# Fetching the next batch's keys and queries one layer earlier, with a third key place and a reordered side schedule, in a fused attention, Fourier-mix and feed-forward kernel

## The chip, the core and the metric

The kernel runs on one core of a Trainium2 chip. A core has five engines that run side by side: TensorE (matmuls and transposes, PE in the profile), VectorE (DVE), ScalarE (ACT), GpSimd (POOL) and SyncE (SP, which here issues most DMA transfers). Each works through its own list of instructions in order and waits for others through semaphores. The metric is the device time of one execution in microseconds.

## The reference

Eight batches of 576 tokens, eight heads of 64 columns. Attention is the linear kind: keys are normalised over the tokens, queries over the columns, and a 64 x 64 product of keys and values stands between them. The result x (576 x 512 per batch) is mixed by a two-dimensional Fourier transform of which the real part is kept; then comes a layer norm and a feed-forward block of two layers (512 to 2048 to 512).

```python
q_s = exp(q - max(q, -1));  q_s = q_s / (sum(q_s, -1) + 1e-9)
k_s = exp(k - max(k, 2));   k_s = k_s / (sum(k_s, 2) + 1e-9)
kv = einsum('bhsd,bhse->bhde', k_s, v)
x = einsum('bhsd,bhde->bhse', q_s, kv)        # then (B,H,S,D) -> (B, S, H*D)
u = x + real(fft(fft(x, axis=1), axis=2))
un = (u - mean(u)) / sqrt(var(u) + 1e-6)
out = u + maximum(un @ w_ch1, 0.0) @ w_ch2
```

## The kernel before

The 576 tokens of a batch are cut into four *own* tiles of 128 tokens, named (c, u) with c and u in 0, 1, and a remainder of 64. The remainders of two batches fill one *shared* tile ("t", b), so even batches have five query tiles and odd ones four. The feed-forward works on nine groups of 512 tokens: the eight batches' own tiles and one group of all shared tiles.

After a start that converts the weights and handles batch 0 and the attention and mixing of batch 1, the program is a list of steps, each with a time in units of the feed-forward's matmul steps. The function `timed` writes eight such **passes** (its argument `order`, 1 to 8). The list is sorted by time, and each engine gets its instructions in that order; nothing reorders them later. Pass n runs the feed-forward of one group and, between its matmuls, the attention, mixing and norm of batch n+1 (passes 1 to 6):

- the first layer (`up`, 56 steps, matmuls at L1171): four jobs of 14 steps. Each uses two weight loads `big<-w1s` of 896 KB. There are four places for streamed weights; `used(n)` says that load n is done with, and issues load n+4 into its place (L449).
- the second layer (`down`, matmuls at L1297 and L1267, 50 steps from pass 2 on): seven-product recursion on blocks; its weights come as `big<-w2d` and `big<-w2s`. The seven products add up in three banks of PSUM, "ba", "bb" and "bc". VectorE forms sums u and s from them (L1141 and L1182 in the first layer, L1304 in the second), and block differences (L1243) that later products read. `single` (L1267) multiplies a unit whole, in two halves i = 0, 1; `add` (L1278) adds a half to x.

Attention of a batch takes four key blocks ("k", b, r). Each is loaded (k by L579 or L585, v by L592 and L593), its maximum taken on VectorE (L620), its exponential on ScalarE (L626), transposed on TensorE (L644, L652), copied to `ks` by ScalarE (L648) and VectorE (L657), and multiplied with v (L669). Keys have two places and values two. The query tiles then follow: load (L696, or four parts and a remainder at L330 and L331 for the shared tile), maximum (L723), exponentials (L729), sums, a multiplication by the reciprocal (L742; tiles with c = u have it after the product instead, at L812), transposes (L750), product (L803), copy to x (L814).

`attention_timed` gives these their times. `start` is 0 in passes 1 and 2 and -7 in passes 3 to 6 (so that the first key is turned before the pass begins), `end` is 45. Key r has its exponential at start + 3.5 r. The own query tiles are spread evenly up to 31.3; their loads stand 6.5 steps ahead. Keys 0 and 1 of the next batch are fetched at the end of `folded`, 12.2 steps after `end`, so at the beginning of the second layer. There a `gate` (L560) follows: a VectorE instruction that writes one element of the new key tile from another tile.

`norm` takes statistics of x (L1005, L1006), a root (L1009), the normalised x (L1034), its transposes (L1040) and copies to `unT` (L1048), and the combinations of `unT` that the recursion of the next pass needs: L398 and L400 on VectorE, L399 on GpSimd, and L401 on VectorE (slot 6).

`store` writes x out. Tiles with c different from u are written through `mirror`, a buffer in DRAM, because their tokens stand in reverse: x to mirror (L1425), and 9 steps later mirror to the output (L1427). Others go directly (L1418).

Of the kernel before, what the change touches and what calls it, by code (L numbers as in the profile page):

```python
# [137 lines left out]
class _Block:  # L138
# [154 lines left out]
    def hold(self):  # L293


        held = {12: [("q", D, 3)] * 3, 15: [("k", S, 2)] * 2 + [("v", NC * P, 2)] * 2}
        for some in held.values():
            for i, (tag, n, bufs) in enumerate(some):
                t = self.work.tile([P, n], F32, tag=tag, name=tag, bufs=bufs)
                self.nc.gpsimd.memset(t[0:1, 0:1], 0.0)  # L300
                some[i] = t[0:1, 0:1]

        def free(f):
            copy = self.nc.vector.tensor_copy
            for t in held.get(f, ()):
                copy(t, self.h0[0:1, f, 0:1])
            if f == 12:

                for w in (self.w1sb[0:1, :, HD::HD], self.w2sb[0:1, 0:4, ::HD]):
                    copy(w, w)  # L310
            if f == NF - 1:
                copy(self.w1sb[0:1, :, 0:1], self.w1sb[0:1, :, 0:1])
        return free
# [183 lines left out]
    def attention_timed(self, b, start, end):  # L497
# [3 lines left out]
        own = [("q", b, c, u) for c in range(2) for u in range(2)]  # L501
        first = start + 14 + 5 * len(tail)
        gap, steps = (end - 13.7 - first) / 3, []
        for i, it in enumerate(keys):
            t = start + 3.5 * i
            steps += at(t - 5.5, self.k_load(it)) + at(t, self.k_exp(it)) + at(t + 4, self.k_turn(it))
            steps += at(t + 7, self.k_times_v(it))
        for it in tail:
            t = start + 14
            steps += at(t - 12, self.t_load(it)) + at(t, self.q_exp(it)) + at(t + 8, self.t_turn(it))  # L510
            steps += at(21 if start < 0 else 35, self.t_fold(it))
        for i, it in enumerate(own):
            t = first + gap * i
            steps += at(t - 6.5, self.q_load(it)) + at(t, self.q_exp(it)) + at(t + 8.7, self.q_turn(it))
            steps += at(t + 11.7, self.q_times_kv(it))
        return steps + at((33 if start < 0 else 39) if tail else 22, self.t_times_kv(b))

# [45 lines left out]
    def k_load(self, it):  # L563
# [9 lines left out]
        if r < 2:  # L573
            return []

        def keys():
            k, v = self.key_places()
            self.live[it] = [k, v]
            self.nc.sync.dma_start(k, self.kT[b, r * P:(r + 1) * P, :])  # L579

        return [(0, keys), (3, lambda: self.values_to(b, r, self.live[it][1]))]

    def keys_to(self, b, r, k, v):
        nc = self.nc
        nc.sync.dma_start(k, self.kT[b, r * P:(r + 1) * P, :])  # L585
        self.values_to(b, r, v)
        self.live["k", b, r] = [k, v]

    def values_to(self, b, r, v):
        nc = self.nc  # L590
        cols = slice(r * P, (r + 1) * P)
        nc.sync.dma_start(v[:, 0:4, :], self.v[b, 0:512, cols].rearrange("(c p) n -> p c n", p=P))  # L592
        nc.sync.dma_start(v[:, 4, :], self.v[b, S - P:, cols])  # L593

    def key_places(self):
        return (self.work.tile([P, S], F32, tag="k", name="k", bufs=2)[:],
                self.work.tile([P, NC, P], F32, tag="v", name="v", bufs=2))

    def keys_from(self, b, t):


        for r in range(2):
            k, v = self.key_places()
            self.keys_to(b, r, k, v)
            self.gate(t, k[0:1, 0:1])
# [242 lines left out]
    def folded(self, b):  # L848
# [33 lines left out]
        def fetch():  # L882
            if b == 0:
                self.folded_at = eo[1][:, NN:]
            elif b + 1 < B:
# [110 lines left out]
    def norm(self, g):  # L996
# [53 lines left out]
        def combine():  # L1050
            if g > 0:
                unT = self.unT[g]
                self.b_side(lambda i: unT[:, i], lambda i: unT[:, i], V, nc.gpsimd, V)
# [10 lines left out]
        else:  # L1064
            for n, i in enumerate((0, 2, 1, 3)):
                put((0, 1, 4, 5)[n], stats, i)
            s = slice(0, 4)
            put(6.5, root, s)
# [6 lines left out]
        put(17.5, combine)  # L1075
        return steps

    def norm_steps(self, g):
# [3 lines left out]
        def make(i):  # L1082
            if not box:
                steps = [s for _, s in self.norm(g)]
                n = len(steps) - 13
# [4 lines left out]
                box.append(steps[-1:])  # L1090
# [68 lines left out]
    def up(self, order, g):  # L1159
# [4 lines left out]
        for j in range(NP // 2):  # L1164
# [26 lines left out]
            steps += at(t, job) + [(t + 2 * len(ORDER) - 0.5, lambda n=base + 2 * j + i: self.used(n)) for i in range(2)]  # L1191
# [26 lines left out]
    def deep_down(self, g, order):  # L1218
# [44 lines left out]
        def single(m, n, name, i, q):  # L1263
            if (i, q) == (0, 0):
                bank(name, HD)
            for p in range(4 * q, 4 * q + 4):
                nc.tensor.matmul(box[name][:, i, :], lhsT=h[p][:, A_AT[m], i * P:(i + 1) * P],  # L1267
                                 rhs=self.stream[n][:, p, :], start=i == 0 and p == 0, stop=p == NP - 1,
# [11 lines left out]
        def half(t, c, u, d):  # L1280
            x = lambda: self.xs[g, u][:, c, d * HD:(d + 1) * HD]
            steps.extend(at(t, self.store(g, c, u, x, d)))
# [23 lines left out]
        def ends(unit, n):  # L1306
# [14 lines left out]
            if n == 3:  # L1321
# [4 lines left out]
                 (5, 3): [(1, into, 1, 1, 5), (2, into, 0, 1, 5), (4, into, 0, 1, 3)]}  # L1326
        n, t = 2 * len(ORDER), 0
        for i, unit in enumerate(order):
            if unit in A_AT:
                w = base + (i if i < 2 else 2 + (len(DEEP) - skip) // 4)  # L1330
                for k in range(4):
                    put(t + 2 * k, single, unit, w, {1: "bb", 2: "bc", 4: "ba"}[unit], k // 2, k % 2)
# [5 lines left out]
                for c in range(2):  # L1338
                    put(t - 4.5 + 4 * c, add, "bc" if unit == 2 else "ba", unit // 4, 0, c)
# [14 lines left out]
        if last:  # L1354
            for c in range(2):
                half(t - 8 + 3.5 + c, c, 1, 1)
                half(t - 8 + 6.5 + c, c, 0, 1)
# [48 lines left out]
    def store(self, g, c, u, x, d=None):  # L1406
# [5 lines left out]
        if not own:  # L1412
            def wait():
                self.later += [lambda r=r, m=m: e.dma_start(m, x()[r]) for r, m in self.shared(self.out, 2 * (2 * u + c))]
            return [(0, wait)]
# [11 lines left out]
        return [(0, there), (9, lambda: e.dma_start(cols(out)[:, ::-1, :], cols(box[0])))]  # L1427
# [3 lines left out]
def kernel(ctx: ExitStack, tc: tile.TileContext, q, kT, v, w1, w2, ft,  # L1431
# [24 lines left out]
    def timed(t, order, g):  # L1456
# [6 lines left out]
        start, end = -7 if order > 2 else 0, 45  # L1463
        steps += at(t, blk.attention_timed(b, start, end)) + at(t + end, blk.folded(b))
# [139 lines left out]
```

## Time and profile before

| what | us |
|---|---|
| median of three timed runs | 1107.89 |
| the three runs | 1104.48, 1111.48, 1107.89 |
| profiled execution, its time | 1113.95 |
| profiled execution, its span | 1112.2 |
| passes 1 to 8 in the profile | 119.3, 123.1, 117.5, 118.0, 122.6, 118.1, 96.5, 102.3 |

The span goes from the first to the last instruction. The start, up to the first matmul of pass 1, is 194.8 us; the eight passes follow without a break. Passes 7 and 8 have no attention beside them. In the views below a line gives the engine, the line of the kernel, the tiles written and read, and durations; "<-" after a bracketed number says what ended a wait.

### The profile page before, as it was taken

The page shows a single profiled execution, that of the slowest core. Times are in us where ns is not written, and L with a number is a line of the kernel's source. Part 1 is how long each engine was busy: PE and PEld are TensorE (multiplying, and loading weights), DVE is VectorE, ACT ScalarE, POOL GpSimd, SP SyncE. Part 2 cuts the span into 40 slices and gives each one's busy share as a digit, 9 for nine tenths or more (in the row PEclk, how much of TensorE's full clock was granted, in tenths as well). Part 3 has the DMA queues.
Part 4 walks back from the last instruction along what each step waited for, and adds up shares of the span by engine and source line. Part 5 has one row for each costly group of instructions (what it writes and reads, how often), then busy time and mean ns, then how long its engine had stood idle before and what let it go on. Part 6 is the DMA issues. An engine that isn't in the chain of part 4 may idle for free.

```text
span 1112.2 us, 16987 instructions
## 1 busy us (share of the span) xinstructions
PE 1062.0 (95%) x6336; PEld 919.4 (83%) x6336; DVE 664.4 (60%) x1313; ACT 412.5 (37%) x1001; POOL 495.8 (45%) x409
## 2 busy tenths in 40 slices
PE   5799989999999999999999998999999999999997
PEld 4644446898888899889988998889988998999896
DVE  6784795665555675667655764768456752472251
ACT  6694434462225214542344233521453132231200
POOL 1064571246313645255534741465426364554343
PEclk9999989999999999999999999999999999999999
DMA  9566686447985466637673666456664565576463
GB/s 304 184 218 187 241 302 213 159 159 244 321 281 193 176 223 226 210 138 249 241 254 142 207 235 217 161 198 230 232 203 154 187 246 194 190 246 214 166 236 123
DMA packets 114913, 236.41 MB, mean 213 GB/s; under 512 B 24320, under 2 KB 76288, under 8 KB 104208
## 3 DMA queue, kind: packets, MB, share of 16 engines
q1 hardware_dynamic: 113032, 234.29, 62.3%
q10 hardware_dynamic: 1800, 1.05, 0.3%
q8 instruction: 50, 0.82, 0.3%
q14 instruction: 31, 0.25, 0.1%
HBM read 200.18 MB, written 39.32 MB: 215 GB/s over the span
## 4 chain that ended last, share of the span: by engine, by line
PE 57%; DVE 7%; DMA 1%; ACT 1%; issue 1%; POOL 1%; SPq 0%; ACTq 0%; DVEq 0%; POOLq 0%
PE bb L1171 11%; PE bb L1297 8%; PE bc L1171 7%; PE ba L1171 7%; PE ba L1297 5%; PE bc L1297 5%; PE bb L1267 3%; DVE big L1243 2%; PE acc L669 2%; PE acc L803 1%; DMA k<-in_kT_dram 1%; PE acc L951 1%; PE tr L1040 1%; PE acc L914 1%; PE acc L917 1%
## 5 line engine op out<-in xcount | busy, mean ns | idle before, releaser
L1171 PE MATMUL bb<-unT,big 128*128 128x256 f32 x768 | 185.4, 381 | 3.8 <-DVE krec L631 2.3
L391 POOL TENSOR_TENSOR big<-big 128x512 f32<-128x512 f32 (+1 forms) x38 | 46.3, 1218 | 283.7 <-ACT big L1183 282.8
L1171 PEld LDWEIGHTS bb<-unT,big 128*128 128x128 f32 x768 | 143.5, 191 | 23.0 <-DVE krec L631 2.7
L1183 ACT ACTIVATE big<-big 128x512 f32<-128x512 f32 x96 | 60.4, 629 | 190.7 <-DVE big L1182 190.3
L1171 PE MATMUL ba<-unT,big 128*128 128x256 f32 x512 | 124.8, 382 | 0.2 <-ACT unT L1048 0.2
L1171 PE MATMUL bc<-unT,big 128*128 128x256 f32 x512 | 123.8, 380 | 0.0
L1297 PE MATMUL bb<-big 128*128 128x128 f32 x848 | 105.6, 276 | 3.2 <-DVE u L1304 3.2
L1141 DVE TENSOR_TENSOR u<-bb,s 128x512 f32<-128x512 f32 x66 | 45.5, 690 | 100.7 <-PE bb L1171 90.8
L1171 PEld LDWEIGHTS ba<-unT,big 128*128 128x128 f32 x512 | 95.3, 192 | 12.3 <-ACT unT L1048 0.5
L1171 PEld LDWEIGHTS bc<-unT,big 128*128 128x128 f32 x512 | 94.6, 190 | 12.1 <-DVE big L1182 0.6
L1297 PEld LDWEIGHTS bb<-big 128*128 128x128 f32 x848 | 99.6, 192 | 4.4 <-DVE u L1304 4.4
L1247 POOL TENSOR_TENSOR x<-x,big 128x512 f32<-128x512 f32 x52 | 76.7, 1484 | 35.9 <-DVE big L1304 18.4
L1243 DVE TENSOR_TENSOR big<-big 128x512 f32<-128x512 f32 x92 | 84.1, 956 | 5.9 <-POOL big L392 3.4
L1297 PE MATMUL ba<-big 128*128 128x128 f32 x640 | 79.6, 275 | 0.0
L1297 PEld LDWEIGHTS ba<-big 128*128 128x128 f32 x640 | 76.4, 192 | 1.2
L729 ACT ACTIVATE q<-q,qm 128x64 f32<-128x64 f32 x240 | 64.7, 338 | 30.5 <-DVE qm L723 23.4
L1243 POOL TENSOR_TENSOR big<-big 128x512 f32<-128x512 f32 x26 | 40.5, 1566 | 63.9 <-DVE big L1243 63.9
L1182 DVE TENSOR_TENSOR big<-bc,u 128x512 f32<-128x512 f32 x64 | 44.0, 687 | 24.7 <-PE bc L1171 23.6
L1304 DVE TENSOR_TENSOR u<-bb,s 128x256 f32<-128x256 f32 x40 | 16.8, 419 | 66.0 <-PE bb L1297 51.0
L1297 PE MATMUL bc<-big 128*128 128x128 f32 x416 | 51.5, 275 | 0.0
L1267 PE MATMUL bb<-big 128*128 128x256 f32 x224 | 51.5, 381 | 0.0
L1297 PEld LDWEIGHTS bc<-big 128*128 128x128 f32 x416 | 48.9, 192 | 0.0
(280 smaller groups left out, 2049.7 us busy)
## 6 DMA issues: line engine op xcount, KB each, us to landing
big<-w2d SPq DMA_DIRECT2D x67, 1024.0 KB
big<-w1s SPq DMA_DIRECT2D x64, 896.0 KB
big<-w2s SPq DMA_DIRECT2D x16, 1024.0 KB
big<-in_w_dram SPq DMA_DIRECT2D x21, 512.0 KB
w2d<-big SPq DMA_DIRECT2D x42, 256.0 KB
q<-in_q_dram SPq DMA_DIRECT2D x27, 256.0 KB
k<-in_kT_dram SPq DMA_DIRECT2D x24, 288.0 KB
v<-in_v_dram SPq DMA_DIRECT2D x24, 256.0 KB
```

Of the source, the lines that this page charges most:

```text
L391: e1.tensor_tensor(out=to(4), in0=at(2), in1=at(3), op=ALU.add)
L669: nc.tensor.matmul(pk, lhsT=ks[:, c, :], rhs=v[:, c, :], start=(c == 0), stop=(c == NC - 1))
L729: nc.scalar.activation(q[:, h, :], q[:, h, :], ACT.Exp, bias=m[:, h:h + 1])
L1141: plus = lambda t: V.tensor_tensor(out=temp(t), in0=box["bb"][:], in1=box["s1"][:], op=ALU.add)
L1171: nc.tensor.matmul(bank()[:, i, :], lhsT=w[:, WA_AT[m], k * P:(k + 1) * P], rhs=self.unT[g][:, B_AT[m], k, :], start=first and i == 0 and ...
L1182: steps = [(0, lambda: V.tensor_tensor(out=hp(i), in0=bank()[:], in1=u()[:], op=ALU.add)), (0.8, lambda: nc.scalar.activation(hp(i), hp(i) ...
L1183: (0.8, lambda: nc.scalar.activation(hp(i), hp(i), ACT.Relu))]
L1243: e.tensor_tensor(out=to(o), in0=to(x), in1=to(y), op=op)
L1247: G.tensor_tensor(out=x, in0=x, in1=tile(m), op=ALU.add)
L1267: nc.tensor.matmul(box[name][:, i, :], lhsT=h[p][:, A_AT[m], i * P:(i + 1) * P], rhs=self.stream[n][:, p, :], start=i == 0 and p == 0, sto ...
L1297: nc.tensor.matmul(box[place[n]][:, i, :], lhsT=own(m)(A_AT[n])[:, f, :], rhs=w[:, r // 2, r % 2 * P:r % 2 * P + P], start=first and f == ...
L1304: V.tensor_tensor(out=out, in0=box[n][:], in1=box[t][:], op=ALU.add)
```

## The change

- **Three places for keys**, and the loads of keys 0, 1, 2 (steps 20 to 22), of values 0 and 1 (35, 36) and of the first two query tiles (46.5, 50) of the next batch are issued in the first layer of the pass before (`ahead`). Key 3 is loaded 5 steps ahead of its exponential, values 2 and 3 1.8 steps behind it. The gates on keys remain only for batch 2, whose first keys still come through `keys_from`.
- **Query tiles** go (0,0), (0,1), (1,1), (1,0). For batch 2 their times, and that of the shared tile, are set by hand; loads stand 6 steps ahead.
- The second **weight load** of each pair in the first layer is issued 5 steps later, save in the last job.
- **Statistics** stand at 0.7, 2.7, 4.7, 6 instead of 0, 1, 4, 5, and the root 0.7 later.
- The **last combination** (slot 6) is a step of its own, 10 steps behind the others.
- In the last pass the second **half** of `single` gets a bank of its own ("bb") for units 2 and 4, and the last mirrored store is issued 0.7 instead of 9 steps after the write of its mirror.

The core of the diff:

```diff
-        held = {12: [("q", D, 3)] * 3, 15: [("k", S, 2)] * 2 + [("v", NC * P, 2)] * 2}
+        held = {12: [("q", D, 3)] * 3, 15: [("k", S, 3)] * 3 + [("v", NC * P, 2)] * 2}
...
-        own = [("q", b, c, u) for c in range(2) for u in range(2)]
+        own = [("q", b, c, u) for c, u in ((0, 0), (0, 1), (1, 1), (1, 0))]
...
+        places = [first + gap * i for i in range(4)]
+        shared = start + 14
+        if tail and start == 0:
+            shared, places = 17, [14, 21, 26, 31.3]
         for i, it in enumerate(keys):
             t = start + 3.5 * i
-            steps += at(t - 5.5, self.k_load(it)) + at(t, self.k_exp(it)) + at(t + 4, self.k_turn(it))
-            steps += at(t + 7, self.k_times_v(it))
+            if i > 1:
+                steps += at(t - (6.5 if b == 2 else 5), self.k_load(it)[:1]) + at(t + 1.8, self.k_load(it)[1:])
+            steps += at(t, self.k_exp(it)) + at(t + 4, self.k_turn(it)) + at(t + 7, self.k_times_v(it))
...
-        for i, it in enumerate(own):
-            t = first + gap * i
-            steps += at(t - 6.5, self.q_load(it)) + at(t, self.q_exp(it)) + at(t + 8.7, self.q_turn(it))
-            steps += at(t + 11.7, self.q_times_kv(it))
+        for t, it in zip(places, own):
+            steps += at(t, self.q_exp(it)) + at(t + 8.7, self.q_turn(it)) + at(t + 11.7, self.q_times_kv(it))
+        loads = [(t, self.q_load(it)) for t, it in zip(places, own)] + [(shared - 6, self.t_load(it)) for it in tail]
+        loads.sort(key=lambda s: s[0])
+        for t, load in loads[2 * (b > 2):]:
+            steps += at(t - 6, load)
...
+    def ahead(self, b):
+        steps = [(20 + r, lambda r=r: self.keys_to(b, r)) for r in range(3)]
+        steps += [(35 + r, lambda r=r: self.values_to(b, r)) for r in range(2)]
+        q = [self.q_load(("q", b, 0, u)) for u in range(2)]
+        if b % 2 == 0:
+            q = [self.t_load(("t", b)), q[0]]
+        return steps + at(46.5, q[0]) + at(50, q[1])
...
-            elif b + 1 < B:
+            elif b == 1:
                 self.keys_from(b + 1, eo[1])
...
-                self.b_side(lambda i: unT[:, i], lambda i: unT[:, i], V, nc.gpsimd, V)
+                for e, to, x, y in ((V, 4, 1, 0), (nc.gpsimd, 1, 3, 1), (V, 5, 3, 4)):
+                    e.tensor_tensor(out=some(to), in0=some(x), in1=some(y), op=ALU.subtract)
+        def combine_last():
+                V.tensor_tensor(out=some(6), in0=some(2), in1=some(5), op=ALU.subtract)
...
-                put((0, 1, 4, 5)[n], stats, i)
+                put((0.7, 2.7, 4.7, 6)[n], stats, i)
...
         put(17.5, combine)
+        put(27.5, combine_last)
...
-            steps += at(t, job) + [(t + 2 * len(ORDER) - 0.5, lambda n=base + 2 * j + i: self.used(n)) for i in range(2)]
+            steps += at(t, job) + [(t + 2 * len(ORDER) - 0.5 + 5 * i * (j < NP // 2 - 1), lambda n=base + 2 * j + i: self.used(n)) for i in range(2)]
...
-            if (i, q) == (0, 0):
+            if q == 0 and (m != 1 or i == 0):
                 bank(name, HD)
...
+        names = {1: ("bb", "bb"), 2: ("bc", "bb"), 4: ("ba", "bb")}
...
-                    put(t + 2 * k, single, unit, w, {1: "bb", 2: "bc", 4: "ba"}[unit], k // 2, k % 2)
+                    put(t + 2 * k, single, unit, w, names[unit][k // 2], k // 2, k % 2)
...
-                half(t - 8 + 6.5 + c, c, 0, 1)
+                half(t - 8 + 6.5 + c, c, 0, 1, 0.7 if c else 9)
...
+        if b + 1 < B:
+            steps += at(t, blk.ahead(b + 1))
         steps += at(t, blk.attention_timed(b, start, end)) + at(t + end, blk.folded(b))
```

## The prediction

> **What bounds the kernel now.** I read the page first (shares of busy time, then the slices), next the waits of TensorE from 190 us on, where the written-out schedule begins, then the waits of VectorE, then the timelines around the two longest stalls.
>
> The page, engines and granted clock:
>
> ```profile
> PE 1062.0 (95%) x6336; PEld 919.4 (83%) x6336; DVE 664.4 (60%) x1313; ACT 412.5 (37%) x1001; POOL 495.8 (45%) x409
> ...
> PEclk9999989999999999999999999999999999999999
> ```
>
> TensorE is busy 95% of the span; no other engine is above 60%. So only TensorE's idle time, its slow clock and the tail after its last matmul can be won. Waits of TensorE after 190 us (total, times, longest):
>
> ```profile
> PE acc L669 <- ACT ks L648: 6.4, 5, 1.9
> PE bb L1297 <- DVE u L1304: 3.2, 5, 1.6
> PE bb L1171 <- DVE krec L631: 2.3, 1, 2.3
> PE bb L1171 <- DVE u L1141: 1.5, 1, 1.5
> ```
>
> The engines named are only the last links. VectorE's own waits, from 190 to 920 us, tell where it starts:
>
> ```profile
> DVE k L560 <- DMA k<-in_kT_dram: 21.9, 10, 4.0
> DVE km L620 <- DMA k<-in_kT_dram: 17.5, 7, 6.1
> ```
>
> VectorE stands 39 us in all on keys that have not landed. The timeline of pass 5 shows how that reaches TensorE (start, length, engine, line; in brackets the idle time before):
>
> ```profile
> 677.72 0.33 SPq L579 DMA_DIRECT2D k<-in_kT_dram  x1
> ...
> 684.09 0.75 DVE L620 TENSOR_REDUCE km<-k 128x1 f32<-128x576 f32 x1 [3.91 <-DMA k<-in_kT_dram]
> ...
> 685.79 0.56 ACT L648 COPY ks<-tr 128x512 f32<-128x512 f32 x1
> ...
> 686.40 1.81 PE L669 MATMUL acc<-v,ks 128*128 128x128 f32 x10 [1.91 <-ACT ks L648]
> ```
>
> The fourth key block is issued at 677.72, because with two places it needs key 1's, whose last transpose ran at 677.38. It lands 6.4 us later, VectorE's maximum stops everything behind it, ScalarE's copy of the third key stands behind the exponential of the fourth, and TensorE waits. After that the clock falls. Windows of 2 us after the same stall in pass 2, then whole first layers of passes 1, 2 and 5 (length, busy times, clock, DMA):
>
> ```profile
> 326.00:328.00 2.00, 0.58 (x3) 0.54 (x4) 1.93 (x5) 1.19 (x3) 0.00 (x0) 1.00 0.96 343
> 328.00:330.00 2.00, 2.00 (x13) 1.94 (x12) 1.64 (x5) 1.49 (x4) 0.00 (x0) 0.70 0.47 174
> 330.00:332.00 2.00, 2.00 (x7) 1.53 (x7) 0.00 (x0) 0.64 (x2) 0.00 (x0) 0.50 0.19 58
> ...
> 314.10:381.40 67.30, 63.48 (x342) 56.17 (x340) 36.98 (x74) 28.26 (x71) 21.58 (x18) 0.97 0.57 191
> ...
> 672.70:740.10 67.40, 63.85 (x342) 55.88 (x340) 41.16 (x85) 29.77 (x78) 27.04 (x24) 0.97 0.51 174
> ...
> 194.80:256.90 62.10, 62.10 (x345) 55.51 (x346) 42.80 (x85) 30.40 (x79) 25.28 (x22) 1.00 0.41 144
> ```
>
> Passes 2 and 5 take over 5 us more than pass 1 for the same matmuls: idle time plus about 2 us of half clock, in which TensorE counts as busy.
>
> **What the Trainium skill says.** "TensorE: Matmul & The Clock Gate", Part 1 (The HAM clock gate): an idle window of about 3.4 us halves the clock until a busy window has passed. The trace agrees on the halving (0.50 at 330 us), though the idle time named there is only 2.3 us; so a stall costs its length and some 2 us more. "SBUF — State Buffer", Who interferes with whom: a VectorE instruction with two SBUF inputs contends with a GpSimd instruction that reads SBUF, one with a single input does not. The trace agrees: the last combination (L401) takes 1.64 us at 671.13 beside L399 on GpSimd, its twins L398 and L400 0.69. "DMA: Bandwidth & Descriptors", Issuing engines are not separate DMA queues: transfers issued by several engines share the same 16 DMA engines and interleave. The trace agrees as far as it goes: ScalarE's last mirrored store kept its 1.8 us while SyncE's direct store ran beside it.
>
> **The change, part by part.** Durations are of the profiled execution, span 1112.2 us.
>
> *Third key place, keys 0 to 2 fetched a pass ahead.* The loads stay 24 of keys, 24 of values; they move. Key 3 now needs key 0's place, free after its last transpose (670.80 in pass 5), and SyncE reaches it after the weight load at 673.35: some 3.9 us earlier than 677.72. VectorE was free for it at 680.18 and stood 3.91 us; landing 3.9 us earlier removes that. Removed: in pass 2, 2.31 idle and 1.9 of slow clock; in pass 5, 1.91 and about 2.2 (its first layer has 5.9 us over 61.5, which is pass 1's 62.1 less key 0's transposes of 0.6 that stand before the layer here; 1.12 of it is counted below and 0.5 are waits of queries). Sum 8.3. I take 7.3, since key 3's load still follows a weight load. Bounds: 0 and 8.3.
>
> *Gates gone.* Twelve L560 gates on keys become two, so ten of under 0.1 us go; what counts is that each made VectorE stand until a key landed (21.9 us in all). Most of it lies beside TensorE's work; in pass 5 it delays L1243, for which TensorE waits 1.02 at 752.92, 1.2 with what follows. I take 1.2; bounds 0 and 1.5.
>
> *Last combination later.* L401 (0.69 to 1.64) stands before the maximum of key 1, that before an exponential, that before the copy for which L669 waits 1.12 us in each of passes 3 to 6. Moved behind, all four go: 4.5. It is first read by the product that starts ten steps into the layer, 3.5 steps (3.9 us) after its new place, against 0.69: free. Bounds 2 and 4.5.
>
> *Query tiles reordered.* In pass 2 the third tile no longer needs VectorE's multiplication (L742, 1.47 us at 356.85), behind which u (L1141) stood while TensorE waited 1.50 at 358.07. The multiplication comes with the last tile, whose result ScalarE then copies (0.57). With the small query waits of passes 3 and 5 (0.37 and 0.15 each) 2.5; I take 1.5, since the new last tile now hands VectorE's work to ScalarE just ahead of the folds. In pass 1 the first own tile moves from step 19 to 14 and the shared one back to 17; each keeps its 8 steps between exponential and transpose, and ScalarE is busy 30.4 of the 62.1 us there: nothing.
>
> *Statistics 0.7 to 1.7 steps later.* One pair (0.86 us) no longer stands before u3 (L1304) in the second layer. The second layers of passes 2, 4 and 6 (odd batches) take 45.9 to 46.0 against 44.0 in pass 3; 1.1 is the shared mix's matmuls, so 0.8 are waits. I take half of it in three passes, 1.2; bounds 0 and 2.4. In pass 7 the 1.61 wait stays: the order ahead of u is the same.
>
> *Own banks for last halves.* Twice in the last pass TensorE waits 0.59 us (1068.74, 1101.51) for VectorE to empty the half of a bank it writes next. With another bank both go: 1.2. The other bank is empty by then: it was copied out at 1065.98, and at 1096.7.
>
> *Last mirrored store earlier.* TensorE ends at 1105.84, the span 6.3 later:
>
> ```profile
> 1102.10 3.72 PE L1267 MATMUL ba<-big 128*128 128x256 f32 x16 [0.59 <-DVE x L1278]
> ...
> 1106.31 0.34 SPq L1418 DMA_DIRECT2D out_dram<-x  x1
> 1106.74 0.67 SPq L1427 DMA_DIRECT2D out_dram<-mirror  x1
> ```
>
> The mirrored store runs from 1108.7 to 1110.6 in 256 B packets, after ScalarE's two (to 1108.5). Issued ahead of the last direct store it overlaps ScalarE's: 2.1 at most, 0 if the DMA engines are full. They are busy to 0.3 in those slices, so I take 1.8.
>
> *Moved loads and what they pass.* On SyncE's queue the three keys, two values and two queries of the next batch leave the second layer's start and stand between weight loads of the first; the second weight load of each pair moves back 5 steps. GpSimd's queue has nothing new but one memset. First layers move 174 to 191 GB/s, second layers 214 to 225, so the loads go where there is room. The delayed weight load has 9.5 steps of 1.11 us (62.1 over 56), 10.5 us; it and what shares those microseconds (a weight load, three keys, a query tile) are 917+885+262 thousand bytes, at 278 GB/s (two weight loads between 696.4 and 703.0) 7.4 us and about 1 to start. That fits, with 2 us to spare. The query loads that go ahead, at steps 46.5 and 50, find their places free: the last transpose is at step 40. I charge 1.7 for some new small wait; bounds 0 and 6.
>
> Sum: 7.3+1.2+4.5+1.5+1.2+1.2+1.8−1.7 = 17.0. The span becomes 1095, and that execution's 1113.95 would be 1097. The timed runs lie lower, 1104.48 to 1111.48, median 1107.89; less 17.0 that is 1091. Part of their lead will be stalls that did not happen, which cannot be won twice, so I go 2 us up: **1093**.
>
> **The rivals.**
> *The wait moves* (0.20). Values keep two places: value 2 still waits for the first product, L669. Its load was issued at 676.27 and ended at 681.3, while TensorE would reach it at 684.5; 3.2 us of slack, and it now stands behind one more weight load and key 3 shares the time. If it, or key 3, is late in the two passes, 2 us plus 2 of clock return in each, 8 of the 17: 1101. For it: the start of these layers is where transfers crowd. Against: no TensorE wait is on a value now.
> *Weights late: slower* (0.08). The mechanism is the delayed second weight load beside the three keys. If the rate falls below 196 GB/s (2,064 thousand bytes in 10.5 us) TensorE waits, and pays 2 us of clock on top, in each of passes 1 to 5. The change loses from 3.4 us per pass, a load 1.4 us late, which is under 173 GB/s. At 4 us late, 30 come against 17: 1121. For it: one weight load took 13 us at 305. Against: that was beside 512 B packets of the second layer's writes, and mid-layer pairs took 6.7.
> *It doesn't do what it says* (0.10): SyncE's queue is served in order and reaches key 3 no earlier than before, or the timed runs hardly had these stalls; only combination, banks and tail (7.5) remain, less 1.7: 1102.
>
> **How the numbers follow.** Forecast 0.62, with 1086 to 1099 around it. The range goes up through the cases at 1101 and 1102 to 1105, leaves the slower one out, and goes down to 1085, where the charge of 1.7 and the 2 us do not come and the upper bounds do in part. A measurement of this kernel tells about 1%, 11 us, from no change, so 1096.8 is the line. Of the forecast's 0.62, some 0.10 lies above it; of the moved wait's 0.20, half lies below it, where it strikes in one pass only (1097 and less). So faster by over 1%: 0.52+0.10 = 0.62; within 1%: 0.10+0.10+0.10 = 0.30; slower by over 1%: 0.08.
>
> **What would show it.** Right: first layers of passes 2 and 5 within 1 us of 62, no clock of 0.5 after 190 us, no key among VectorE's waits over 1 us, no 1.12 waits at L669, TensorE's end to span's end near 4.5. Wrong: TensorE waiting for weights in mid-layer, or for values.

## The result and the profile after

| | before | after |
|---|---|---|
| timed median, us (4 runs each) | 1108.44 (1104.48 to 1111.48) | 1095.04 (1093.67 to 1096.52) |
| ratio, 95% interval | | 0.9881 [0.9846, 0.9917] |
| span of the profiled execution, us | 1112.2 | 1094.3 |

The change is 13.4 us faster in the timed runs, and 17.9 us between the two profiled executions. The forecast was 1093.0. Lines of the code have moved: before and after, L620 and L628 are the key's maximum, L669 and L677 the product with v, L1171 and L1186 the first layer, L1297 and L1312 the second, L1267 and L1282 `single`, L579 and L596 a key's load, L1427 and L1443 the store out of the mirror, L1418 and L1434 the direct store.

Shares of busy time on the page after, and TensorE's granted clock by slice:

```profile
PE 1057.3 (97%) x6336; PEld 918.2 (84%) x6336; DVE 662.2 (61%) x1304; ACT 413.8 (38%) x1001; POOL 484.8 (44%) x410
...
PEclk9999989999999999999999999999999999999999
```

Waits of TensorE from 190 us on, in the changed kernel (total, times, longest):

```profile
PE bb L1312 <- DVE u L1319: 2.2, 2, 1.6
PE tr L758 <- DVE q L750: 0.7, 2, 0.4
PE acc L811 <- ACT qT L768: 0.3, 2, 0.2
PE ba L1186 <- ACT unT L1056: 0.2, 1, 0.2
```

This is the whole list. The 6.4 us at the product with v, the 2.3 at `krec` and the 1.5 at u are gone; the 1.6 us wait of pass 7 that the prediction left standing stands. VectorE has no wait on a key among its waits of this stretch in this execution. The windows of the first layers of passes 2 and 5 (length, busy TensorE, weight loads, VectorE, ScalarE and GpSimd, clock, DMA share, GB/s):

```profile
315.18:376.64 61.46, 61.46 (x341) 54.81 (x340) 36.71 (x75) 28.20 (x71) 21.20 (x18) 1.00 0.67 223
663.96:726.12 62.16, 61.63 (x342) 54.63 (x340) 39.06 (x80) 29.11 (x76) 26.58 (x24) 1.00 0.59 203
```

They took 67.30 and 67.40 before. Key 3 of pass 5, in the timeline (start, length, engine, line):

```profile
662.37 0.33 SPq L596 DMA_DIRECT2D k<-in_kT_dram  x1
...
664.50 0.74 DVE L628 TENSOR_REDUCE km<-k 128x1 f32<-128x576 f32 x1
...
669.96 0.74 DVE L628 TENSOR_REDUCE km<-k 128x1 f32<-128x576 f32 x1
```

It is issued 1.6 us before the pass begins (before: 5.0 us after), so 7.6 us ahead of its maximum, which no longer waits.

One part went the other way. The end of the changed kernel, whose TensorE ends at 1086.78:

```profile
1084.82 2.10 ACTq L1443 DMA_DIRECT2D out_dram<-mirror  x2
1086.24 0.67 SPq L1443 DMA_DIRECT2D out_dram<-mirror  x1
1086.81 0.42 DVE L1293 TENSOR_TENSOR x<-bb,x 128x256 f32<-128x256 f32 x1 [2.96 <-PE bb L1282]
1087.27 1.98 SPq L1434 DMA_DIRECT2D out_dram<-x  x1
```

and its windows (the last two columns are the DMA share and GB/s; the direct store's packets are among those of the second window):

```profile
1086.78:1089.48 2.70, 0.00 (x0) 0.00 (x0) 0.42 (x1) 0.00 (x0) 0.00 (x0) 1.00 0.27 61
1089.48:1091.59 2.11, 0.00 (x0) 0.00 (x0) 0.00 (x0) 0.00 (x0) 0.00 (x0) 0.87 0.46 119
1091.59:1092.60 1.01, 0.00 (x0) 0.00 (x0) 0.00 (x0) 0.00 (x0) 0.00 (x0) 0.50 0.30 73
```

The SyncE store out of the mirror is issued ahead of the direct store, as intended, but the direct store's issue then takes 1.98 us instead of 0.34, and three mirrored stores still fill the time from 1086.45 to 1092.68. From TensorE's end to the span's end it is 7.5 us, against 6.3 before and 4.5 forecast. Of the signs that the prediction named for being right, the lengths of the first layers, the clock (1.00 from 190 us to TensorE's end), VectorE's waits on keys and the waits at the product with v came; the end did not.

### The profile page after: what moved, and what is told of

Its sections match the earlier page's. It is cut to its first block, busy times and chain, and to the rows that moved or that the text cites. A ratio compares the mean times of both kernels' runs of the same rounds, so it can differ in the third digit from the quotient of the medians.

```text
span 1094.3 us, 16985 instructions
## 1 busy us (share of the span) xinstructions
PE 1057.3 (97%) x6336; PEld 918.2 (84%) x6336; DVE 662.2 (61%) x1304; ACT 413.8 (38%) x1001; POOL 484.8 (44%) x410
## 4 chain that ended last, share of the span: by engine, by line
PE 82%; DVE 3%; ACT 1%; issue 1%; POOL 1%; POOLq 0%; DVEq 0%; ACTq 0%
PE bb L1186 15%; PE bb L1312 10%; PE ba L1186 9%; PE bc L1186 9%; PE bc L1312 6%; PE ba L1312 6%; PE bb L1282 4%; PE acc L677 2%; PE acc L811 2%; PE bb L1397 2%; PE bc L1131 2%; PE acc L922 2%; PE acc L925 2%; PE acc L959 1%; PE bc L1397 1%; PE ba L1397 1%
## 5 line engine op out<-in xcount | busy, mean ns | idle before, releaser
L1186 PE MATMUL bb<-unT,big 128*128 128x256 f32 x768 | 184.1, 380 | 0.0
L1186 PEld LDWEIGHTS bb<-unT,big 128*128 128x128 f32 x768 | 142.9, 190 | 18.8 <-DVE unT L1062 0.4
L1186 PE MATMUL ba<-unT,big 128*128 128x256 f32 x512 | 123.9, 380 | 0.2 <-ACT unT L1056 0.2
L1186 PE MATMUL bc<-unT,big 128*128 128x256 f32 x512 | 123.9, 380 | 0.0
L1312 PE MATMUL bb<-big 128*128 128x128 f32 x848 | 105.2, 276 | 2.2 <-DVE u L1319 2.2
L1186 PEld LDWEIGHTS ba<-unT,big 128*128 128x128 f32 x512 | 94.7, 190 | 12.3 <-ACT unT L1056 0.5
L1186 PEld LDWEIGHTS bc<-unT,big 128*128 128x128 f32 x512 | 94.5, 190 | 12.1 <-DVE big L1197 0.9
L1312 PEld LDWEIGHTS bb<-big 128*128 128x128 f32 x848 | 99.7, 192 | 2.9 <-DVE u L1319 2.9
L1262 POOL TENSOR_TENSOR x<-x,big 128x512 f32<-128x512 f32 x52 | 68.0, 1318 | 28.0 <-ACT big L1289 14.8
L1312 PE MATMUL ba<-big 128*128 128x128 f32 x640 | 79.6, 275 | 0.0
L1312 PEld LDWEIGHTS ba<-big 128*128 128x128 f32 x640 | 76.4, 192 | 1.2
L1282 PE MATMUL bb<-big 128*128 128x256 f32 x256 | 58.7, 381 | 0.0
L1282 PEld LDWEIGHTS bb<-big 128*128 128x128 f32 x256 | 48.3, 190 | 7.9 <-DVE big L1197 1.1
L1312 PE MATMUL bc<-big 128*128 128x128 f32 x416 | 51.5, 275 | 0.0
```

Of the source, the lines that this page charges most:

```text
L1186: nc.tensor.matmul(bank()[:, i, :], lhsT=w[:, WA_AT[m], k * P:(k + 1) * P], rhs=self.unT[g][:, B_AT[m], k, :], start=first and i == 0 and ...
L1262: G.tensor_tensor(out=x, in0=x, in1=tile(m), op=ALU.add)
L1312: nc.tensor.matmul(box[place[n]][:, i, :], lhsT=own(m)(A_AT[n])[:, f, :], rhs=w[:, r // 2, r % 2 * P:r % 2 * P + P], start=first and f == ...
```

## The experiments

In all of them the timed median of the kernel before was 1108.2 to 1108.6. Lengths of first layers run from the first matmul of the layer to that of `single`. The start ahead of pass 1 took between 193.5 and 197.0 us in the fourteen profiled executions, so single times and spans don't tell differences of that size; the lengths of layers do. From the start of pass 1 to TensorE's last matmul it was 911.0 us before and 891.2 in the changed kernel.

**1. The kernel before, profiled again.**

> The kernel before, profiled a second time. Theory (late keys are a matter of how transfers happen to interleave): the 1.12 us waits at L669 in passes 3 to 6 and the two 0.59 us waits in pass 8 come back to 0.1 us, since they follow from the order of instructions; but the waits of VectorE for keys (39 us in the first profile) differ by several us, and the first layers of over 67 us fall on other passes than 2 and 5, or on fewer. Rival (late keys are fixed by the schedule): passes 2 and 5 again, 67.3 and 67.4 us within 0.5.

Span 1111.1, one timing. Pass 5's first layer took 63.54 us instead of 67.38, with no stall at key 3; pass 2's took 70.26 instead of 67.26. The four 1.1 us waits at L669 came again. So the late fourth key of pass 5, on which the prediction modelled the stalls, is an accident of one execution: none of those of experiments 1 to 3 and 6 to 8 had it. Pass 2's stall recurs, and the key that stops VectorE there is the third, as two lines of the kernel before already show:

```profile
319.18 0.33 SPq L579 DMA_DIRECT2D k<-in_kT_dram  x1
...
325.89 0.75 DVE L620 TENSOR_REDUCE km<-k 128x1 f32<-128x576 f32 x1 [6.14 <-DMA k<-in_kT_dram]
```

The fourth key, issued at 324.30, made nobody wait: its maximum at 328.94 has no wait in front of it.

**2. The third key place alone**, in the kernel before.

```diff
...
-        return (self.work.tile([P, S], F32, tag="k", name="k", bufs=2)[:],
+        return (self.work.tile([P, S], F32, tag="k", name="k", bufs=3)[:],
```

> The kernel before with a third key place and nothing else: keys 0 and 1 still come at the start of the second layer with their gates, key 2 no longer waits for a place, key 3 waits for key 0's. Theory (the place is what is missing): no wait of VectorE for a key at L620 over 1 us, first layers of passes 2 and 5 at 61.5 to 63.5, gates still some 20 us of VectorE's waits, span about 1104 (1112.2 less 8.3). Rival (the fetch a pass ahead is needed, since at the start of a layer transfers crowd): at least one first layer of 65 us or more, span 1108 or more.

1108.42, ratio 0.9998 [0.9984, 1.0012]: nothing, against the theory. Pass 3, which begins at 433.23, shows why key 3 hardly moves (4.7 us into the pass, 5.0 before):

```profile
436.79 0.39 SPq L592 DMA_DIRECT2D v<-in_v_dram  x1
...
437.90 0.38 SPq L579 DMA_DIRECT2D k<-in_kT_dram  x1
...
441.22 0.75 DVE L620 TENSOR_REDUCE km<-k 128x1 f32<-128x576 f32 x1 [0.53 <-DMA k<-in_kT_dram]
```

Value 2 stands ahead of key 3 on SyncE's queue and waits for its own place, until the first product has read value 0 (435.38 to 436.76). Key 3 has a place and can't be issued.

**3. The third place, and key 3 ahead of value 2.**

```diff
-            steps += at(t - 5.5, self.k_load(it)) + at(t, self.k_exp(it)) + at(t + 4, self.k_turn(it))
+            steps += at(t - 5, self.k_load(it)[:1]) + at(t - 1.2, self.k_load(it)[1:])
+            steps += at(t, self.k_exp(it)) + at(t + 4, self.k_turn(it))
...
```

> The kernel before with three key places and one more edit: a key's load stands 5 steps ahead of its exponential and its values' load 1.2 steps ahead of it, so that key 3 stands ahead of value 2 on SyncE's queue. Gates, fetching at the layer's end, combination, query order and tail as before. Theory (the third place alone was worth nothing because value 2, waiting for its place, stood ahead of key 3 in the in-order queue): key 3 is issued 3 to 4 us earlier than in the kernel with the place alone, VectorE's waits on keys at the maximum fall from 11.3 us to under 4, none over 1.5 us, first layers of passes 2 and 5 take 62 to 63.6 us, and the timed ratio is 0.993 to 0.998. Rival (keys 0 to 2 must be fetched a pass ahead too, since the crowd at the start of the layer is what makes key 3 late): VectorE's waits stay above 8 us and the ratio is 0.998 to 1.002. Second rival (values now come late): TensorE waits at the product L669/L670 on v by over 1 us and the ratio is over 1.0.

1109.24, ratio 1.0004 [0.9987, 1.0021]. Key 3 went out 1.6 us before pass 3 began (434.53, the pass at 436.12) instead of 4.7 us after, and no maximum waited for it, but the time stayed: the theory failed again. So the queue's order explained why key 3 was late, and key 3 was not what the time was lost to. VectorE's one wait left on a key's maximum is the third key of pass 2, and it reaches TensorE:

```profile
318.23 2.66 SPq L580 DMA_DIRECT2D k<-in_kT_dram  x2
...
326.45 0.75 DVE L621 TENSOR_REDUCE km<-k 128x1 f32<-128x576 f32 x1 [5.33 <-DMA k<-in_kT_dram]
...
327.99 1.13 PE L1172 MATMUL bb<-unT,big 128*128 128x256 f32 x4 [1.51 <-DVE krec L632]
```

**4. The changed kernel with value 2 ahead of key 3 again.**

```diff
-... + at(t + 1.8, self.k_load(it)[1:])
+... + at(t - 3, self.k_load(it)[1:])
```

> The changed kernel with one edit: values 2 and 3 are loaded 3 steps ahead of their key's exponential instead of 1.8 steps behind it, so value 2, which waits for its place until the first product, stands ahead of key 3 on SyncE's queue again; three key places and keys fetched a pass ahead stay. Theory (the order on the queue decides): key 3 is issued 3 to 5 us later than in the changed kernel, VectorE waits for key 3 by 1 to 4 us in at least three passes, TensorE's waits grow by 1 to 6 us, and the timed ratio to the kernel before goes from 0.988 to 0.990 to 0.996. Rival (the keys fetched ahead are what counts; key 3 has slack): no wait on a key over 1 us and 0.987 to 0.989.

1095.41, ratio 0.9879 [0.9852, 0.9905]. VectorE waits for key 3 again, 3.4 and 3.2 us in passes 1 and 2 and 0.5 to 1.2 in 3 to 6, and no layer is longer for it. The rival holds for the time, though not for the waits: key 3 has slack. (VectorE's 3.1 and 3.4 us of waiting for key 3 of pass 2 in experiments 9 and 10, which fetch as the changed kernel does, say the same: TensorE has no wait on it in either.)

**5. The changed kernel with two key places** (keys 0 and 1 fetched ahead).

```diff
...
-        steps = [(20 + r, lambda r=r: self.keys_to(b, r)) for r in range(3)]
+        steps = [(20 + r, lambda r=r: self.keys_to(b, r)) for r in range(2)]
...
-        steps = [] if b > 2 and r < 3 else [(0, lambda: self.keys_to(b, r))]
+        steps = [] if b > 2 and r < 2 else [(0, lambda: self.keys_to(b, r))]
...
-        k = self.work.tile([P, S], F32, tag="k", name="k", bufs=3)[:]
+        k = self.work.tile([P, S], F32, tag="k", name="k", bufs=2)[:]
```

> The changed kernel with two key places: keys 0 and 1 a pass ahead, keys 2 and 3 when a place is free. Theory (the place is what is missing): VectorE waits for keys 2 and 3 again, 10 us or more in all, and at least one first layer takes 65 us or more; span 1098 to 1104. Rival (two keys out of the way at the start of the layer are enough): VectorE's waits for keys under 4 us, all first layers of passes 2 to 6 under 63, span 1094 to 1096.

1101.90, ratio 0.9949 [0.9933, 0.9966], 6.9 us above the changed kernel's median. TensorE now waits 4.6 us for values, in four places (longest 2.8), and VectorE 13.4 us for keys: keys 2 and 3 wait for the places of keys 0 and 1, and the values stand behind them on the queue. In pass 3 key 3 goes out at 437.06, after key 1's last transpose at 436.71, and value 2 at 438.30, 4.9 us into the pass instead of 2.2. The longest wait, with the windows during and after it:

```profile
446.58 1.35 PE L677 MATMUL acc<-v,ks 128*128 128x128 f32 x10 [2.75 <-DMA v<-in_v_dram]
```

```profile
446.00:448.00 2.00, 1.42 (x13) 1.45 (x14) 0.03 (x1) 0.00 (x0) 0.00 (x0) 1.00 0.84 281
448.00:450.00 2.00, 2.00 (x13) 1.77 (x12) 0.83 (x3) 1.54 (x4) 0.00 (x0) 1.00 0.64 194
```

The clock stays at 1.00, and the layer is 3.0 us longer than in the changed kernel (65.15 against 62.15). So the third place is worth something once the loads are fetched ahead, and nothing by itself. This is also the only run in which the prediction's moved wait, on values, appears.

**6. The kernel before without its gates from batch 3 on.**

```diff
-            self.gate(t, k[0:1, 0:1])
+            if b == 2:
+                self.gate(t, k[0:1, 0:1])
```

> The kernel before without the gates on keys of batches 3 to 7. Theory: VectorE's 21.9 us of waits at the gates fall to the two of batch 2 (4.7), but TensorE gains only where a gate stood ahead of L1243: the second layer of pass 5 falls from 45.3 to 44.0, the others stay within 0.2, about 1.2 us in all. Rival: VectorE's time there is worth more, second layers of passes 2, 4 and 6 fall too (45.9 to 45.4 or less).

1107.95, one timing. The second layer of pass 5 took 44.00 instead of 45.26. But the same layer took 44.04, 44.01 and 44.00 in experiments 2, 3 and 7, which have the gates, and 45.26 in experiment 1: the gate costs 1.25 us when the key is late there, in three of the six profiled executions that have it (the third is experiment 8). The second layers of passes 2, 4 and 6 kept their lengths, against the rival.

**7. The last combination alone**, in the kernel before.

```diff
-                self.b_side(lambda i: unT[:, i], lambda i: unT[:, i], V, nc.gpsimd, V)
+                for e, to, x, y in ((V, 4, 1, 0), (nc.gpsimd, 1, 3, 1), (V, 5, 3, 4)):
+                    e.tensor_tensor(out=some(to), in0=some(x), in1=some(y), op=ALU.subtract)
...
+        put(27.5, combine_last)
...
```

> The kernel before with one edit: the last combination (slot 6) is a step of its own, 10 steps behind the other three. Theory of the prediction: the four 1.1 us waits at L669 in passes 3 to 6 go, 4.5 us, ratio 0.9955 to 0.9965. Rival (the second key's maximum waits for the key's landing anyway, or the exponential is late for another reason): waits of 0.5 us or more stay at L669 in these passes, and the ratio is 0.998 to 1.000. In the changed kernel passes 4 and 6, which hold none of the late keys, became 1.5 us shorter in the first layer; the combination alone should give 1.1 of these.

1104.64, ratio 0.9956 [0.9940, 0.9972]. First layers of passes 3 to 6: 62.54, 60.81, 62.64 and 60.81, against 63.54, 62.20, 63.55 and 62.20 in experiment 2, together 4.7 us; no wait at the product with v is left. This execution also had the worst pass 2 of all (70.78; third key 8.7 us late).

**8. Everything but the fetching**: the changed kernel with the keys' and values' loads where the kernel before has them, two places, and the gates (query loads at the new tiles' own times).

```diff
...
-        steps = [] if b > 2 and r < 3 else [(0, lambda: self.keys_to(b, r))]
-        return (steps or [(0, lambda: None)]) + [(0, lambda: self.values_to(b, r))]
+        return [(0, lambda: self.keys_to(b, r)), (3, lambda: self.values_to(b, r))]
...
-            elif b == 1:
+            elif b + 1 < B:
...
-        if b + 1 < B:
-            steps += at(t, blk.ahead(b + 1))
```

> The changed kernel with its fetching undone: keys and values are loaded where the kernel before loads them (two key places, 5.5 steps ahead of the exponential, keys 0 and 1 of the next batch at the second layer's start with their gates), queries at their own times; combination, query order, statistics, weight delay, own banks and mirrored store stay changed. Theory (fetching ahead with a third place is worth what the single parts leave over): the parts that stay give 4 (combination) + 1.7 (banks) + 1.7 (statistics and query waits of the second layers) + 1 to 2 (queries), less 1.2 (tail), 7 to 8 us, so 1100.5 to 1102, ratio 0.993 to 0.9945, with VectorE's gates standing 20 us again and pass 2's first layer at 63.5 us or more. Rival (the fetch is worth nothing in the timed runs): 1094.5 to 1097.

1099.31, ratio 0.9925 [0.9902, 0.9948], a little under what the theory said; by the medians the fetch of keys, values and queries, with the gates, is worth 4.3 us of the change. The intervals of the two ratios still touch; in the profiles it is 3.4, of which 1.9 lie in the first layer of pass 2, 1.25 at the gate of pass 5 and 0.2 in pass 3. Experiment 5 was no faster than this (1101.90): fetching ahead with two places gains nothing over not fetching ahead. VectorE's waits on keys, then TensorE's longer waits:

```profile
DVE k L574 <- DMA k<-in_kT_dram: 22.4, 10, 3.8
DVE km L625 <- DMA k<-in_kT_dram: 19.7, 11, 5.4
```

```profile
PE bb L1309 <- DVE u L1316: 2.2, 2, 1.6
PE bb L1183 <- DVE krec L636: 1.6, 1, 1.6
PE bb L1309 <- DVE unT L1255: 1.0, 1, 1.0
```

VectorE stands 42 us on keys, more than the 39 of the kernel before, and TensorE feels two waits of it: 1.6 in pass 2 and 1.0 at the gate in pass 5. Once the combination no longer stands between the keys, their lateness in passes 3 to 6 is hidden, but for that gate and 0.2 us in pass 3.

**9. The changed kernel with the old query order.**

```diff
-        own = [("q", b, c, u) for c, u in ((0, 0), (0, 1), (1, 1), (1, 0))]
+        own = [("q", b, c, u) for c, u in ((0, 0), (0, 1), (1, 0), (1, 1))]
```

> The changed kernel with the query tiles in their old order (0,0), (0,1), (1,0), (1,1). The prediction's step: VectorE's multiplication for the third tile stands before u again and TensorE waits 1.5 us in pass 2, with 0.4 and 0.15 in passes 3 and 5; first layer of pass 2 63 us (from 61.46), passes 3 and 5 62.3 to 62.5 (from 62.15), span 2 us longer. Rival (in pass 2 it is the tiles' new times, set by hand, or the keys, and not the order): pass 2 stays within 0.4 us of 61.46.

1097.3, one timing. TensorE's 1.5 us wait for u is back, and the first layer of pass 2 takes 63.04 instead of 61.46; passes 4 and 6 are 0.11 longer and pass 1 0.4 (62.74 instead of 62.33), passes 3 and 5 the same.

**10. The changed kernel with its last mirrored store last.**

```diff
-                half(t - 8 + 6.5 + c, c, 0, 1, 0.7 if c else 9)
+                half(t - 8 + 6.5 + c, c, 0, 1)
```

> The changed kernel with its last mirrored store issued 9 steps behind the mirror's write, as in the kernel before. The prediction's step (1.8 us won by issuing it early): TensorE's end to the span's end 9 us or more, from 7.5, and 1.8 us slower. Theory after the changed kernel's trace (three mirrored stores in a row set the end, and the early one only takes its share from the two of ScalarE and holds up the direct store): 7.0 to 7.8 us, and the time within 0.6 us of the changed kernel's, on either side.

1096.07, ratio 0.9883 [0.9843, 0.9923]; 7.4 us from TensorE's end to the span's end, against 7.5 with the store early. The end shows nothing of the 1.8 us forecast, and the medians, 1.0 us apart, are within the spread.

**11. The changed kernel without the reversal at the end**: the last pass's halves that go through the mirror are stored directly, so the reversal of their tokens is left out.

```diff
-        if c == u:
+        if c == u or d is not None:
             return [(0, lambda: e.dma_start(out, x()))]
```

> The changed kernel with the halves of the last pass that go through the mirror stored directly instead, so that the reversal of the tokens in these halves is left out. Theory (the end of the changed kernel is bound by its three mirrored stores, which move 256 B packets at about 72 GB/s and take 6.1 us in a row whatever their order): TensorE's last matmul to the span's end falls from 7.5 to 3 to 4.5 us, and the span from 1094.3 to 1090 to 1091.5. Rival (the end is set by the last addition, the fixed cost of any store and the closing instructions): it stays at 6.5 to 7.5 us.

TensorE ends at 1088.11 and the span at 1091.4, 3.2 us later instead of 7.5 (one timing, 1093.13). The mirrored stores set the end, as the theory said.

**12. Mirrored stores of the last pass in 16 strips of 16 columns.**

```diff
-        cols = lambda a: a.rearrange("t (k n) -> k t n", n=DH)
+        cols = lambda a: a.rearrange("t (k n) -> k t n", n=DH if d is None else 16)
```

> The changed kernel with the mirrored stores of the last pass's halves cut into 16 strips of 16 columns instead of 4 of 64: four times as many packets, of 64 B instead of 256 B. Theory (a store is spread over as many DMA engines as its outermost dimension counts, here 4 of 16, and a packet takes as long as its bytes): the DMA share in the tail rises from 0.3 to near 1, a mirrored store takes 0.6 to 1 us instead of 2, TensorE's end to the span's end falls from 7.5 to 4 to 5 us, the time by 2.5 to 3.5. Rival (a packet of 64 B costs as much as one of 256 B): the share rises to near 1 with 128 packets per engine as before, so a store takes 2 us again and the end stays at 7 to 8, the three now in a row. Second rival (64 B writes are slow in themselves): the end grows past 9 us.

1094.11, ratio 0.9866 [0.9835, 0.9898], and 6.1 us from TensorE's end to the span's end. No theory hit the size. The window of the tail reads

```profile
1086.60:1089.00 2.40, 0.00 (x0) 0.00 (x0) 0.00 (x0) 0.00 (x0) 0.00 (x0) 0.89 1.41 125
```

(the share exceeds 1 because packet records overlap: up to 33 of one queue run at once). The Trainium skill, "DMA: Bandwidth & Descriptors", Rules for kernel authors, says that an outermost dimension smaller than 16 confines a transfer to at most that many DMA engines. The share agrees: 0.32 of 16 with four strips, full with 16. This window holds the direct store too; between 1085.00 and 1085.50 ScalarE's mirrored stores ran alone, with a share of 1.24 and 119 GB/s, against 0.32 and 72 for a store of four strips. So four times the share brings 1.65 times the rate: a 64 B packet took 11 ns (median), where one of 256 B took 18. The end is 1.4 us shorter than the changed kernel's; the timed runs (1092.82 to 1095.47 against 1093.67 to 1096.52) overlap and do not settle it.

## Why the prediction was right, step by step

The total was right, 1093 against 1095.04, and so was the sign. The single terms were 5.6 us too large together, most of it in two of them; the 1.7 us held back for a new wait and the 2 us held back for stalls that would not recur took up 3.7 of that. That the total came so near is owed to these allowances as much as to the terms. The prediction's numbers, and what the runs put in their place:

| step | predicted, us | measured, us |
|---|---|---|
| third place and keys ahead | 7.3 | 3.7 on average (timed: fetch 4.3 with the gates) |
| gates gone | 1.2 | 1.25 when it strikes, in 3 of 6 |
| last combination later | 4.5 | 4.7 in the profile; timed 3.9 |
| query order | 1.5 | 1.5 |
| statistics later | 1.2 | 1.7 in the layers named; not isolated |
| own banks | 1.2 | 0.86 of 1.72 |
| last mirrored store earlier | 1.8 | 0 |
| charge for a new wait | −1.7 | 0: no new wait of TensorE |

**Keys: right effect, wrong key, too large.** The step that failed is "landing 3.9 us earlier removes that", which charges both stalls to key 3. A third place alone does not bring key 3 earlier (experiment 2), since value 2 blocks the queue. With the values moved behind it, key 3 does go out earlier, in pass 5 of the changed kernel by 6.6 us; but that changes nothing in the time, whether it is done in the kernel before (experiment 3) or undone in the changed one (experiment 4). What costs is the third key of pass 2, loaded at the layer's start. Fetching it in the pass before removes that, and the third place is what makes room for it (experiment 5). The cost is uneven. The wait of VectorE on that key, the stall of TensorE that follows, and the length of pass 2's first layer over the one with keys fetched ahead and the same query order (63.04, experiment 9; 61.46, the changed kernel, for experiment 8):

| execution | key late | TensorE idle | layer longer |
|---|---|---|---|
| experiment 2 | 5.1 | 1.3 | 1.5 |
| experiment 6 | 5.3 | 1.5 | 1.8 |
| experiment 3 | 5.3 | 1.5 | 1.8 |
| experiment 8 | 5.4 | 1.6 | 1.9 |
| before | 6.1 | 2.3 | 4.2 |
| experiment 1 | 8.0 | 4.2 | 7.2 |
| experiment 7 | 8.7 | 4.9 | 7.7 |

The mean over these related kernels is 3.7 us. That "a stall costs its length and some 2 us more" held for the stalls of 1.9 and 2.3 us on which it was built, and not for the shorter ones. The profile on which the prediction was built also had pass 5's accident, 3.8 us more than experiment 1 there. This is most of why the change saved 17.9 between two profiles and 13.4 in the timed runs. The prediction saw this possibility and put 2 us on it; it was 4.5.

**Combination: right**, by itself and at its size. Its effect on the keys was larger than the step said: in experiment 8 it also hides late keys.

**Queries: right.** 1.58 in pass 2 and 0.11 in passes 4 and 6, less 0.27 by which pass 1 is longer than before (62.33 against 62.06), is 1.5.

**Gates and statistics.** The gate's mechanism was right, and its effect a draw. Second layers of passes 2, 4 and 6 took 45.35, 45.35 and 45.47 instead of 45.92, 45.93 and 46.04; every kernel with the later statistics shows these lengths within 0.01 us, every one without them the longer ones, but no run changed them alone.

**Own banks and tail: the term that was wrong.** The two `single` stages became 0.86 us shorter each (14.67 to 13.81 and 7.93 to 7.07). The first gain stays. The second is lost, because the end is set by the mirrored stores (experiment 11): from the start of the last `single` to the span's end it was 14.4 us on average in the six executions with the old end and 14.4 in the five with the new one. "Issued ahead of the last direct store it overlaps ScalarE's" happened, and gained nothing, since two such stores together move no more than one. DMA packets in one microsecond, first with both in flight (changed kernel, 1090.5 to 1091.5 us; q10 is ScalarE's queue, q1 SyncE's), then with SyncE's alone (before, 1109 to 1110; packets, MB, share):

```profile
DMA packets 283, 0.07 MB, mean 72 GB/s; under 512 B 283, under 2 KB 283, under 8 KB 283
q10 hardware_dynamic: 187, 0.05, 21.0%
q1 hardware_dynamic: 96, 0.02, 10.7%
```

```profile
DMA packets 283, 0.07 MB, mean 72 GB/s; under 512 B 283, under 2 KB 283, under 8 KB 283
q1 hardware_dynamic: 283, 0.07, 31.8%
```

The 119 GB/s of the changed kernel's second window are no more of the mirrored stores: 96 of its packets are the direct store's, of 1 KB. The prediction read the DMA share of 0.3 as room; for a second store of four strips it was none.

**The rivals.** The moved wait did not come: no TensorE wait on a value is left (only experiment 5 has it). "It doesn't do what it says" was half right, on both its grounds: with the third place alone key 3 went out hardly earlier, and the timed runs had less of these stalls than the profile; the fetch ahead and the combination carried the gain all the same. The slower one, late weights, never came either: no wait on a weight appears among TensorE's waits, though the first layer of pass 2 moves 223 GB/s instead of 191.

The sum of the measured terms, 3.7 (third key) + 0.6 (the gate, half the time) + 4.7 + 1.5 + 1.7 + 0.86, is 13.1, against 13.4 timed. Passes 3 and 5 are another 0.4 and 0.5 us shorter in the changed kernel than in experiment 7, which would make it 14.0; which part did that stays open. In pass 5 it is not the fetch and not the query order (62.16 in experiments 8 and 9 too). The later weight loads, the queries' new times and the later statistics were not run alone. The timed runs also draw together, from 7.0 us between lowest and highest before to 2.9, which fits the removal of an uneven stall; so does the stretch from the start of pass 1 to TensorE's last matmul, 903.3 to 911.0 us in the executions of experiments 1 to 3 and of the kernel before, and 891.1 to 891.2 in those of the changed kernel and of experiments 4 and 10 to 12.

## What to carry to other kernels

A long stall in one profiled execution may be a draw: profile the kernel before a second time, and price the stall that recurs. Waits of a helper engine are not time: 42 us of them cost 2.6 here, and what decides is whether the wait is passed on. When stores set the end, look at whether two of them in flight move more than one before trying to reorder them.

## What the runs showed of the hardware

- **The recorded length of a TensorE stall did not alone decide whether the clock fell.** Stalls of 1.3 to 1.6 us left the clock at 1.00 and cost 1.5 to 1.9. In the kernel before, 1.9 us in pass 5 and 2.3 us in pass 2 halved it for some 3.4 us and cost 3.8 and 4.2; 4.2 and 4.9 us (experiments 1 and 7) cost 7.2 and 7.7. But 2.75 us in experiment 5 left it at 1.00 and cost 3.0. The Trainium skill, "TensorE: Matmul & The Clock Gate", Part 1 (The HAM clock gate), gives an idle window of about 3.4 us; here stalls of 1.9 and 2.3 us halved the clock and one of 2.75 us did not, and the measurement decides. What else decides was not tested. The clock after the stall of pass 5:

```profile
688.00:690.00 2.00, 2.00 (x8) 1.82 (x8) 0.64 (x3) 0.84 (x3) 0.00 (x0) 0.50 0.65 182
```

- **Two stores of four strips in flight together move no more than one**: 283 packets and 72 GB/s in a microsecond in both cases, at a DMA share of 0.32.
- **A store behind a narrow one on the same queue is held up at issue**: 1.5 to 2.0 us for a direct store behind SyncE's mirrored one in the five executions with four strips, 0.8 with 16 strips, and 0.34 in every execution in which it stood ahead.
- **The landing of the same 288 KB key varies**: from the issue of the third key of pass 2 to the maximum that stood waiting for it, the seven executions of the table took from 5.9 us (experiment 6) to 8.9 us (experiment 7).
